# Where a small attention and feed-forward kernel gets its first keys and queries: two of four start-up loads move from the hardware queues to GpSimd's casting queue

## The chip, the cores and the metric

The kernel runs on one core of a Trainium2 chip. A core has a matrix engine (TensorE, "PE" in the profile, with its weight loads as "PEld"), a vector engine (VectorE, "DVE"), an engine for activation functions (ScalarE, "ACT"), a general engine (GpSimd, "POOL") and a synchronising engine (SyncE, "SP"). They run side by side, each through its own instructions in order, and wait for each other through semaphores. Sixteen DMA engines move data between the main memory (HBM) and the on-chip memory (SBUF). A DMA is issued by an engine: by SyncE or ScalarE in what the profile calls a hardware queue (q1 for SyncE, q10 for ScalarE), by GpSimd in the software queue (q0). [...] TensorE writes to PSUM, from where VectorE or ScalarE copy.

The metric is the device time of the whole launch in microseconds (us). Lower is better.

## The reference

Sparse attention over a batch of 4 with 8 heads, 768 positions and head size 64, followed by a feed-forward layer without a residual:

```python
def _attn_ref(q, k, v, n_global, n_local):      # 8 and 96
    scores = scale * np.matmul(q, k.transpose(0, 1, 3, 2))
    rel = pos[:, None] - pos[None, :]
    is_global = pos[None, :] < int(n_global)
    is_local = (rel >= 0) & (rel < int(n_local))
    keep = is_global | is_local
    dist = np.where(is_global & ~is_local, float(n_local), np.abs(rel))
    scores = scores - slopes[:, None, None] * dist[None, :, :]
    scores = np.where(keep, scores, -1000000000.0)
    a = np.exp(scores - np.max(scores, axis=-1, keepdims=True))
    a = a / (np.sum(a, axis=-1, keepdims=True) + 1e-09)
    return np.matmul(a, v)

def _moe_ref(x, w_in, w_out, s, b):             # 3072 x 512, 512 -> 2048 -> 512
    r = np.maximum(x @ w_in, 0.0)
    return (s * (r * r) + b) @ w_out
```

## The kernel before

The tokens are cut into twelve granules of 256 positions (two blocks of 128), three to a batch. A granule goes through attention in units of two heads (four units to a granule; unit `u` is `2` heads of granule `u // 4`), then through the feed-forward layer. Every engine's order of work is written out by hand: the program switches the automatic scheduling off, so that the order of the calls is the order on each engine.

The keys and queries have to be laid out as head size by position before TensorE can use them. The memory gives them as position by head size, so each pair of heads is transposed by TensorE (with an identity matrix, lines 331 and 345) and copied out of PSUM into the tiles `kx` and `qx`.

**The first granule** has a start of its own. Four hardware loads bring its keys and queries in float32 (line 129): SyncE issues the keys and ScalarE the queries, heads 0 to 3 first, then heads 4 to 7, 256 KB each. A partition holds two neighbouring positions, so that each piece read is 512 bytes long. They go into four buffers of the tag `first`. `cast_first(h2, n, copy)` (line 262) turns one of them into bfloat16 and lays it out in the granule's tile `nat[0]`; `h2` is the half of the heads, `n` is 0 for keys and 1 for queries, and `copy` says on which engine, `cp` being VectorE and `acp` ScalarE. `qk_first(h2, n, evac)` (line 325) makes the four transposes of that part, and `evac` copies the result out (line 335).

**All the other loads** are GpSimd's. In the order of their issue: keys and queries of granule 1's first block (`load_qk(1, 0)`), the values of granule 0 (`load_v(0)`, one load to a block), keys and queries of granule 1's second block, and then slices of `w_in` with the values of granule 1 between them, `w_out`, and granules 2 and 3. The issue itself keeps GpSimd busy for most of a microsecond (lines 102, 108, 116, 140 and 146).

**The opening** (lines 1014 to 1048) starts with ten matmuls on constants (`warm`, line 159) while the first loads are on their way. Heads 0 to 3 are cast, transposed and copied out; `open_bias` adds the distance bias of units 0 and 1 by a matmul (line 420), and their scores follow (line 445). Then come the exponentials (`expo`, line 454, on ScalarE), four more warm matmuls, and heads 4 to 7 in the same way for units 2 and 3. After that, granule 1's keys and queries are transposed (line 345), the probabilities are multiplied with the values (`stage_A`, line 499), and the feed-forward layer of granule 0 begins (line 623). `make_koff` (line 387) copies keys for the offset blocks of granule 1.

The scores of units take turns in two PSUM buffers (`sc`), and the transposes and the feed-forward products in three (`psh`). The pool `gpool` has two buffers of the tag `gT`, 16 KB a partition each, which hold the hidden layer of two granules.

Of the kernel before, what the change touches and what calls it, by code (L numbers as in the profile page):

```python
# [8 lines left out]
F32 = mybir.dt.float32  # L9
BF16 = mybir.dt.bfloat16  # L10
# [7 lines left out]
def kernel(  # L18
# [13 lines left out]
    nc = tc.nc  # L32
    P = nc.NUM_PARTITIONS

    B, H, S, D = q.shape
# [4 lines left out]
    GB = 2  # L40
# [17 lines left out]
    work = ctx.enter_context(tc.tile_pool(name="work", bufs=3))  # L58
    ppool = ctx.enter_context(tc.tile_pool(name="ppool", bufs=4))
    gpool = ctx.enter_context(tc.tile_pool(name="gpool", bufs=2))  # L60
# [21 lines left out]
    def nat_tile(j):  # L82
        if j not in nat:
            nat[j] = ldp.tile([P, 2, GB, H, D], BF16, name="nat", tag=f"nat{j % 4}", bufs=1)
        return nat[j]

    srcs = (k, q)

    def rows_of(src, b, sb):
        return src[b, :, sb * P : (sb + 1) * P, :].rearrange("h p d -> p h d")  # L90

    def pairs_of(src, j, h0=0, nh=H):

        b, g = divmod(j, NGR)
        return src[b, h0 : h0 + nh, g * GT : (g + 1) * GT, :].rearrange(
            "h (p s) d -> p h (s d)", s=GB
        )

    def load_qk(j, i):
        b, g = divmod(j, NGR)  # L100
        for n in range(2):
            nc.gpsimd.dma_start(nat_tile(j)[:, n, i, :, :], rows_of(srcs[n], b, g * GB + i))

    def load_v(j, blocks=range(GB)):
        b, g = divmod(j, NGR)
        for i in blocks:
            sb = g * GB + i
            nc.gpsimd.dma_start(vbuf[b % 2][:, sb, :, 0:D], rows_of(v, b, sb))  # L108
# [13 lines left out]
        nc.gpsimd.tensor_copy(g[0:1, :], ap)  # L122


    first_f32 = {}
    for h2 in range(2):
        for n, eng in enumerate((nc.sync, nc.scalar)):
            f = work.tile([P, H // 2, GB * D], F32, name="first", tag="first", bufs=4)
            eng.dma_start(f[:], pairs_of(srcs[n], 0, h2 * H // 2, H // 2))
            first_f32[h2, n] = f  # L130
    nc.scalar.preload_act_table_set("natural_log_exp_and_others")

    w_in_bf = const.tile([P, KC, DF], BF16, name="w_in_bf")
# [22 lines left out]
    def warm(n, w=2 * P):  # L156
        ps = ps_h.tile([P, w], F32, name="ps_w", tag="psh")
        for _ in range(n):
            nc.tensor.matmul(
                ps[:],  # L160
                lhsT=nc.const_aps.tensor(1.0, (P, P), BF16),
                rhs=nc.const_aps.tensor(1.0, (P, w), BF16),
                start=True,
                stop=True,
            )
# [6 lines left out]
        nc.sync.dma_start(b_bc[:], moe_b.to_broadcast((P, 1)))  # L172


    rel_2 = gpool.tile([P, 2, 2 * P], F32, name="rel", tag="gsum2", bufs=1)
    rel, far = rel_2[:, 0, :], rel_2[:, 1, :]
    nc.gpsimd.iota(
# [20 lines left out]
    nc.vector.tensor_scalar_max(base_bf[0:NG, 0, :], base_bf[0:NG, 0, :], -float(NL))  # L198
    nc.vector.memset(base_bf[0:NG, 2, :], -float(NL))
    nat_tile(0)  # L200
    load_qk(1, 0)
    load_v(0)
    load_qk(1, 1)
# [58 lines left out]
    def cast_first(h2, n, copy):  # L262
        hs = slice(h2 * H // 2, (h2 + 1) * H // 2)
        copy(  # L264
            nat[0][:, n, :, hs, :],
            first_f32[h2, n][:].rearrange("p h (s d) -> p s h d", s=GB),
        )


# [6 lines left out]
    gT = {}  # L276
# [6 lines left out]
    def qk_of(b, n):  # L283

        if b not in qk:
            qk[b] = (
                qkp.tile([P, NB, HP, P + (NG + 15) // 16 * 16], BF16, name="kx", tag="kx"),
                qkp.tile([P, NB, HP, P], BF16, name="qx", tag="qx"),
            )
        return qk[b][n][:, :, :, 0:P]  # L290
# [34 lines left out]
    def qk_first(h2, n, evac):  # L325

        ps = ps_h.tile([P, GB, 2, P], BF16, name="ps_t", tag="psh")
        for i in range(GB):
            for c in range(2):
                hp = 2 * h2 + c  # L330
                nc.tensor.transpose(  # L331
                    ps[:, i, c, :], nat[0][:, n, i, 2 * hp : 2 * hp + 2, :], ident_bf[:]
                )
        dst = qk_of(0, n)[:, 0:GB, 2 * h2 : 2 * h2 + 2, :]
        evac(
            dst.rearrange("p b c (m s) -> p c b m s", s=GB),
            ps[:].rearrange("p s c (b m) -> p c b m s", b=GB),
        )
# [534 lines left out]
    def evac(pr, n):  # L873

        ps3 = prod_ps[pr, n][:]
        ps = ps3.rearrange("p a c -> p (a c)")
        if n == 1:
            res[pr] = [
                work.tile([P, GB, CH], F32, name=f"part{i}", tag=f"part{i}", bufs=1)
                for i in range(3)  # L880
            ]
            res[pr].append(out_tile() if pr == NJ // 2 - 1 else res[pr][0])
        r0, r1, r7, r6 = (t[:].rearrange("p a c -> p (a c)") for t in res[pr])
        if n == 1:
            scaled(res[pr][0][:], ps3, both_blocks(bvec[:, 0:CH]))
        elif n == 2:
            store(pr, 0, 0, ps, r0)
        elif n == 5:
            scaled(res[pr][1][:], ps3, both_blocks(bdiff[:]))
        elif n == 6:  # L890
            scaled(r6, ps, r0)
        elif n == 7:
            nc.scalar.activation(r7, ps, ACT.Copy, scale=s_bc[:])
        elif n == 3:
            store(pr, 0, 1, ps, r1)
        elif n == 4:
            store(pr, 1, 0, ps, r6)
# [43 lines left out]
    def run(cs):  # L941
        for c in cs:
            c()
# [54 lines left out]
    cp = nc.vector.tensor_copy  # L998
    acp = nc.scalar.copy
    u = {}  # L1000

    def open_bias(us):
        for i in us:
            u[i] = stage_S(i)
            u[i][0]()
# [7 lines left out]

    warm(10, 4 * P)
    cast_first(0, 0, cp)
    cast_first(0, 1, acp)
    for h in range(6, H):
        nc.vector.tensor_scalar_mul(diag[:, h, :], ident_bf[:], slopes[h] / QSCALE)
    qk_first(0, 0, cp)
    qk_first(0, 1, acp)  # L1020
    open_bias((0, 1))
    cast_first(1, 0, cp)
    cast_first(1, 1, acp)
    for part in range(2):
        for i in (0, 1):
            u[i][1](part)
    run(u[0][2])
    warm(4)
    qk_first(1, 0, cp)
    qk_first(1, 1, acp)  # L1030
    run(u[1][2])
    open_bias((2,))
    open_scores((2,))
    make_koff(1, [0])
# [223 lines left out]
```

The softmax here doesn't subtract the row's maximum and nothing guards it: scores larger than these inputs give would overflow.

## Time and profile before

| | |
|---|---|
| time, median of 6 runs | 208.43 us (208.33 to 208.74) |
| the profiled execution's own time | 208.33 us |
| its span, first to last instruction | 206.5 us |
| granted TensorE clock | 1.00 |
| TensorE / VectorE / ScalarE / GpSimd busy | 202.1 / 160.7 / 128.5 / 69.7 us |
| landing of the four first loads | keys 4.36, queries 4.81; then keys 6.02, queries 6.74 us |
| first packet of GpSimd's queue | 5.58 us (first issue at 1.34) |
| read from HBM, written to it | 27.26 MB, 6.29 MB |

Times within the span are counted from its start. "L264" is line 264 of the kernel. In a group of the profile, `nat<-first` says which tile is written and which is read. A busy TensorE is not TensorE at its peak: matmuls are pipelined and their ends are modelled. The chain of work that ended last is followed back from the last instruction, at each step to whatever released it. A DMA queue's share is the time that its packets took, as a share of 16 engines' time, and packets overlap, so that it can exceed 100%.

### The profile page before, as it was taken

To read this page: it belongs to the slowest core of one execution; us is meant where nothing else is said; L and a number is where in the kernel's file an instruction comes from. 1 tells how busy PE (TensorE), PEld (TensorE's weight loads), DVE (VectorE), ACT (ScalarE), POOL (GpSimd) and SP (SyncE) were. 2 spreads that over 40 slices of the span, in tenths; PEclk is the share of its full clock that TensorE was granted. 3 is DMA by queue.
4 is the path that set the end of the run, shared out by engine and by line. 5 is a ranking of instruction groups with operands and counts; after the bars stand their busy time and mean duration, and the time that the engine had idled before them with its cause. 6 is when DMAs were issued, how large, how long until landed. Compare 5 with 4: busy or idle time off the path is not lost.

```text
span 206.5 us, 5324 instructions
## 1 busy us (share of the span) xinstructions
PE 202.1 (98%) x2192; PEld 160.2 (78%) x2192; DVE 160.7 (78%) x337; ACT 128.5 (62%) x198; POOL 69.7 (34%) x90
## 2 busy tenths in 40 slices
PE   8999999999999999999999999999999999999993
PEld 2678884557867585878888898888888889888883
DVE  7786589977989866799799975699866696737974
ACT  5875669486976558685664595763695764476200
POOL 8985333999355400912700918200000000000000
PEclk9999999999999999999999999999999999999999
DMA  6999999999999999999999999994460300240006
GB/s 166 172 179 201 207 207 177 155 153 136 112 151 135 158 120 229 155 206 237 145 180 164 125 144 214 181 210 57 53 206 3 99 8 0 62 144 0 0 10 197
DMA packets 110836, 28.17 MB, mean 136 GB/s; under 512 B 97852, under 2 KB 109308, under 8 KB 110812
## 3 DMA queue, kind: packets, MB, share of 16 engines
q0 software_dynamic: 76000, 13.11, 86.6%
q1 hardware_dynamic: 33612, 14.13, 39.3%
q10 hardware_dynamic: 1200, 0.59, 1.1%
q8 instruction: 17, 0.28, 0.6%
q14 instruction: 7, 0.06, 0.1%
HBM read 27.26 MB, written 6.29 MB: 162 GB/s over the span
## 4 chain that ended last, share of the span: by engine, by line
PE 96%; DMA 2%; DVE 1%; ACT 0%; issue 0%
PE ps L623 41%; PE ps L823 24%; PE ps L671 14%; PE ps_s L445 6%; PE ps_av L499 5%; DMA first<-in_k_dram 2%; PE ps_t L355 1%; PE ps_s L521 1%; PE ps_x L595 1%; PE ps_s L536 1%; PE ps_t L331 1%; PE ps_av L562 1%; PE ps_t L345 0%; PE ps_s L420 0%; PE ps_last L823 0%; DVE nat L264 0%
## 5 line engine op out<-in xcount | busy, mean ns | idle before, releaser
L623 PE MATMUL ps<-xT,w_in_bf 128*128 128x256 bf16 x768 | 90.3, 273 | 0.0
L633 ACT ACTIVATE gT<-ps 128x512 bf16<-128x512 f32 x96 | 55.8, 599 | 46.7 <-PE ps L623 46.2
L623 PEld LDWEIGHTS <-w_in_bf 128*128 128x128 bf16 x768 | 73.0, 98 | 9.4 <-DVE xT L598 0.2
L454 ACT ACTIVATE pt<-ps_s 128x1024 bf16<-128x1024 f32 (+1 forms) x44 | 39.3, 948 | 2.7 <-PE ps_s L445 2.7
L671 PE MATMUL ps<-w_out_bf,gT 128*128 128x512 bf16 x128 | 29.7, 380 | 0.0
L461 DVE TENSOR_TENSOR pt<-pt,tmpl 128x1024 bf16<-128x1024 bf16 (+1 forms) x40 | 24.5, 646 | 3.6 <-ACT pt L454 3.5
L823 PEld LDWEIGHTS <-gsum 128*128 128x128 bf16 x256 | 24.1, 98 | 3.7 <-DVE gsum L786 0.5
L108 POOL DMA_DIRECT2D vb<-in_v_dram x24 | 21.4, 910 | 5.3 <-DMA w_out_bf<-in_moe_w_out_dram 3.4
L797 DVE TENSOR_TENSOR gT<-gT 128x1024 bf16<-128x1024 bf16 x20 | 13.7, 686 | 11.7 <-ACT gT L633 11.7
L671 PEld LDWEIGHTS <-gT 128*128 128x128 bf16 x128 | 11.7, 98 | 13.0
L470 DVE TENSOR_TENSOR xn<-ps_av,rc 128x256 bf16<-128x256 f32 x48 | 20.4, 425 | 1.7
L823 PEld LDWEIGHTS <-gT 128*128 128x128 bf16 x200 | 18.6, 98 | 2.3
L469 DVE RECIPROCAL rc<-ps_av 128x4 f32<-128x4 f32 x48 | 8.8, 183 | 12.2 <-PE ps_av L499 10.3
L499 PEld LDWEIGHTS <-pt 128*128 128x128 bf16 x320 | 14.4, 97 | 2.7 <-DVE xn L470 0.7
L116 POOL DMA_DIRECT2D nat<-in_k_dram x14 | 12.6, 901 | 8.7 <-DMA nat<-in_k_dram 4.0
L636 DVE TENSOR_TENSOR gT<-gT 128x512 bf16<-128x512 bf16 x32 | 12.8, 421 | 3.5 <-ACT gT L633 3.3
L499 PE MATMUL ps_av<-vb,pt 128*128 128x65 bf16 x208 | 15.4, 193 | 0.0
L823 PE MATMUL ps<-w_out_bf,gsum 128*128 128x256 bf16 x128 | 15.3, 273 | 0.0
L823 PE MATMUL ps<-wsub,gsum 128*128 128x256 bf16 x128 | 15.1, 273 | 0.0
L823 PE MATMUL ps<-w_out_bf,gT 128*128 128x256 bf16 x120 | 13.9, 273 | 0.0
L122 POOL COPY gate<-xT 1x1 bf16<-1x1 bf16 x6 | 1.1, 188 | 37.1 <-DMA xT<-xn 37.1
L116 POOL DMA_DIRECT2D nat<-in_q_dram x14 | 12.4, 886 | 3.0 <-DMA w_in_bf<-in_moe_w_in_dram 1.7
(111 smaller groups left out, 232.0 us busy)
## 6 DMA issues: line engine op xcount, KB each, us to landing
out_dram<-o_q SPq DMA_DIRECT2D x15, 256.0 KB, 2.4
vb<-in_v_dram POOLq DMA_DIRECT2D x24, 128.0 KB, 8.9
nat<-in_k_dram POOLq DMA_DIRECT2D x22, 128.0 KB, 6.7
nat<-in_q_dram POOLq DMA_DIRECT2D x22, 128.0 KB, 6.8
w_out_bf<-in_moe_w_out_dram POOLq DMA_DIRECT2D x4, 512.0 KB, 16.3
w_in_bf<-in_moe_w_in_dram POOLq DMA_DIRECT2D x4, 256.0 KB, 7.5
w_in_bf<-in_moe_w_in_dram POOLq DMA_DIRECT2D x2, 512.0 KB, 11.5
out_dram<-o_sb SPq DMA_DIRECT2D x4, 256.0 KB, 6.9
```

Source lines behind the costliest of these rows:

```text
L108: nc.gpsimd.dma_start(vbuf[b % 2][:, sb, :, 0:D], rows_of(v, b, sb))
L116: nc.gpsimd.dma_start(t[:, n, i, :, :], rows_of(srcs[n], b, sb))
L454: nc.scalar.activation(pt[:, :, 0:ncol], ps[:, :, 0:ncol], ACT.Exp, scale=QSCALE)
L461: nc.vector.tensor_tensor(pv, pv, m.rearrange("p h a c -> p h (a c)"), ALU.mult)
L470: nc.vector.tensor_tensor(dst, av[:, :, :, 0:D], rc[:].to_broadcast((P, 2, 2, D)), ALU.mult)
L499: nc.tensor.matmul(av[:, i, hi, 0 : D + 1], lhsT=pt[:, hi, c * P : (c + 1) * P], rhs=vv, start=(n == 0), stop=(n == len(terms) - 1),)
L623: nc.tensor.matmul(ps[:, i, :], lhsT=w_in_bf[:, kc, fc * P : (fc + 1) * P], rhs=xT[j][:, kc, :], start=(kc == 0), stop=(kc == KC - 1),)
L633: nc.scalar.activation(gs, ps[:], ACT.Relu)
L636: nc.vector.tensor_tensor(gs, gs, gs, ALU.mult)
L671: nc.tensor.matmul(po[:], lhsT=g_of(j)[:, fc, tb * P : (tb + 1) * P], rhs=w_out_bf[:, fc, :], start=(fc == 0), stop=(fc == FC - 1),)
L797: outs.append(lambda: nc.vector.tensor_tensor(gs, gs, gs, ALU.mult))
L823: nc.tensor.matmul(ps[:, tb, cs], lhsT=stat[:, fc, tb * P : (tb + 1) * P], rhs=mov[:, fc, cs], start=(fc == 0), stop=(fc == NH - 1),)
```

## The change

The keys and queries of heads 4 to 7 of the first granule no longer come by the hardware queues. GpSimd loads them with two casting DMAs, ahead of all its other loads, as bfloat16 into a tile `later`, which takes one of the two `gT` buffers. The layout in it is the loads' own (head, then two positions), so `cast_first` for this half is a copy from bfloat16 to bfloat16; both copies are VectorE's now, and so are both copies of the transposes out of PSUM. The exponential of unit 1 is called ahead of them, and the four warm matmuls are split into two ahead of the transposes and two behind.

```diff
-    first_f32 = {}
-    for h2 in range(2):
-        for n, eng in enumerate((nc.sync, nc.scalar)):
-            f = work.tile([P, H // 2, GB * D], F32, name="first", tag="first", bufs=4)
-            eng.dma_start(f[:], pairs_of(srcs[n], 0, h2 * H // 2, H // 2))
-            first_f32[h2, n] = f
+    first_half = {}
+    for n, eng in enumerate((nc.sync, nc.scalar)):
+        f = work.tile([P, H // 2, GB * D], F32, name="first", tag="first", bufs=4)
+        eng.dma_start(f[:], pairs_of(srcs[n], 0, 0, H // 2))
+        first_half[0, n] = f[:]
+    later = gpool.tile([P, 2, H // 2, GB * D], BF16, name="later", tag="gT")
+    for n in range(2):
+        first_half[1, n] = later[:, n]
...
+    def load_later():
+        for n in range(2):
+            nc.gpsimd.dma_start(later[:, n], pairs_of(srcs[n], 0, H // 2, H // 2))
...
     nat_tile(0)
+    load_later()
     load_qk(1, 0)
     load_v(0)
...
             nat[0][:, n, :, hs, :],
-            first_f32[h2, n][:].rearrange("p h (s d) -> p s h d", s=GB),
+            first_half[h2, n].rearrange("p h (s d) -> p s h d", s=GB),
...
     open_bias((0, 1))
     cast_first(1, 0, cp)
-    cast_first(1, 1, acp)
     for part in range(2):
         for i in (0, 1):
             u[i][1](part)
     run(u[0][2])
-    warm(4)
+    run(u[1][2])
+    cast_first(1, 1, cp)
+    warm(2)
     qk_first(1, 0, cp)
-    qk_first(1, 1, acp)
-    run(u[1][2])
+    qk_first(1, 1, cp)
+    warm(2)
     open_bias((2,))
```

## The prediction

> **What bounds the kernel now.** I read the page first. TensorE is busy for 98% of the span, and the chain of work that ended last is 96% TensorE. So nothing can be won or lost except where TensorE waits, and the second view, the chain in order of time, says where that is: only ahead of 8.9 us.
>
> ```profile
> span 206.5 us, 5324 instructions
> PE 202.1 (98%) x2192; PEld 160.2 (78%) x2192; DVE 160.7 (78%) x337; ACT 128.5 (62%) x198; POOL 69.7 (34%) x90
> PE 96%; DMA 2%; DVE 1%; ACT 0%; issue 0%
> ```
>
> The same chain, cut to 4.3 to 10.5 us (start, length, what):
>
> ```profile
> 4.38 0.88 DVE nat L264
> ...
> 5.30 0.76 PE ps_t L331 x8
> 6.06 0.65 PE ps_s L420 x4
> ...
> 6.74 0.51 PE ps_s L445 x12
> 7.25 0.55 PE ps_w L159 x4
> 7.80 0.46 PE ps_t L331 x8
> ...
> 8.28 0.59 ACT qx L335
> ...
> 8.92 0.34 PE ps_s L445 x6
> ```
>
> Three things other than TensorE stand in it: the landing of the first keys (4.36) with VectorE's cast of them, and ScalarE's copy of the second half's queries, which ends at 8.87 and lets unit 2's scores start at 8.92. From there to the end the chain is TensorE's alone: a delay at 8.92 goes to the end in full, and an earlier start does too, if the data come.
>
> The third view is the queues. GpSimd's queue (q0) feeds everything after the first loads, and is the tight resource. Two stretches of the DMA view, 5.0 to 5.5 and then 5.5 to 6.1 us (packets, MB, share):
>
> ```profile
> q10 hardware_dynamic: 227, 0.12, 96.7%
> q1 hardware_dynamic: 70, 0.03, 25.6%
> ```
> ```profile
> q0 software_dynamic: 320, 0.04, 106.5%
> q10 hardware_dynamic: 199, 0.09, 67.4%
> ```
>
> GpSimd issues its first load at 1.34, yet q0 moves nothing before 5.58. ScalarE's q10 closes its last load on the 16 engines one by one from 5.58 to 6.03, and q0 starts on each just then. From there q0 has no gap over 0.4 us before 81 us. Its landings are just in time: the second block of values lands at 10.27 (issue 4.09 plus 6.18) and TensorE's first use is at 10.42; block 1's queries land at 11.91 for 12.00; the fourth eighth of w_in at 19.52 for 19.72. A q0 stream later by more than about 0.1 us stalls TensorE.
>
> The fourth view is the timeline of VectorE beside GpSimd:
>
> ```profile
> 3.23 1.77 POOL L108 DMA_DIRECT2D vb<-in_v_dram  x2
> ...
> 5.83 0.92 POOL L102 DMA_DIRECT2D nat<-in_q_dram  x1
> ```
> ```profile
> 4.38 0.86 DVE L264 CAST nat<-first 128x512 bf16<-128x512 f32 x1 [0.25 <-DMA first<-in_k_dram]
> ...
> 6.48 0.52 DVE L264 CAST nat<-first 128x512 bf16<-128x512 f32 x1
> ```
>
> The same cast takes 0.86 and 0.52. Both end 0.25 after GpSimd's running issue ends (4.99 and 6.75): a copy from SBUF to SBUF that starts well inside an issue waits for its end. Those starting less than 0.24 into one do not wait (line 197, 0.20).
>
> **The change, part by part.** The sum is made against the profiled execution: span 206.5, time 208.33, so 1.83 lies around it; it is 0.10 under the median of 208.43, which I add at the end.
>
> *The two hardware loads of heads 4 to 7 go.* Their packets ran from 4.0 to 6.03. The first two loads close at 3.52 to 3.88 (keys) and 3.90 to 4.26 (queries), before or just as the removed ones begin, so I leave their landings at 4.36 and 4.81. ScalarE's issue of 0.61 goes too; its table load comes 0.6 sooner, but it then waited 0.35 for the queries anyway: nothing.
>
> *Two casting loads ahead in q0.* Each has 512 packets of 256 B. q0 moved 619 packets of 128 B in 0.5 us (0.81 ns each), and 116 of 512 B in 0.3 (2.59 ns). Between them, 256 B comes to 1.40 ns, 0.72 us a load and 1.44 for both. The ends are 0.83 and 2.65 for both. q0 can start when ScalarE's first load closes, at 3.90 to 4.26 instead of 5.58 to 6.03: 1.7 sooner. Everything behind in q0 (keys and queries of granule 1, values, w_in, w_out) moves by 1.44 - 1.70 = -0.26, ends -0.87 and +0.95. I take -0.26; being early is worth nothing, as TensorE is not waiting for it.
>
> *Issues on GpSimd.* Two more, 0.74 each (the w_in issues of as many pieces start 0.74 apart, 6.70 to 7.44) and 0.15 for the first, as now (1.34 to 2.36 where others take 0.87). All later issues move by 1.63. The fourth load behind them (values) is then issued at 5.58; with 1.58 from issue to first packet (114.15 to 115.73, where q0 was empty) it could move from 7.2, and its turn comes at 8.0: hidden by 0.8. If that cover went, each 0.1 would come out at the values' use.
>
> *Landing of the later half.* q0 takes 0.76 from a load's last closing packet (6.88) to its landing (7.64). Keys: 4.26 + 0.72 + 0.76 = 5.74, queries 6.46. VectorE is busy until 6.5, so neither is waited for.
>
> *First cast.* GpSimd's issues now start at 1.34, 2.23, 2.97, 3.84 and 4.71. The cast of the first keys starts at 4.38, well inside the fourth, and ends 0.25 after 4.74, at 4.99 instead of 5.25. The keys' transposes come 0.25 sooner; the queries' do not (cast on ScalarE to 5.45), so scores 0 and 1 start some 0.14 sooner, at 6.60. Ends: 0 and -0.35.
>
> *Two layout copies on VectorE instead of a cast each on VectorE (0.52) and ScalarE (0.62).* 128x512 bf16 to bf16: 0.28 alone and 0.47 with a wait (line 387). They run from 6.3 to at most 7.4, while TensorE does scores 0 and 1 and the warm matmuls to about 7.3: hidden. Ending 0.3 later, they would push what follows one for one.
>
> *Warm matmuls 2 and 2 instead of 4.* Two fewer ahead of the transposes: 2 x 0.114 = -0.23. The two behind run while TensorE waits for the copies: nothing.
>
> *Both copies out of PSUM on VectorE.* Line 335 takes 0.69 there (0.59 on ScalarE), and now one follows the other. Before: the keys' transposes end at 8.02, ScalarE ends at 8.87. After: scores at 6.60 + 0.44 to the warm matmuls + 0.23 + 0.38 for the keys' transposes = 7.65; + 0.04, 0.61 and 0.69 = 8.99; unit 2's scores at 9.04. That is **+0.12** against 8.92, and +0.26 if the first cast gains nothing. Behind them on VectorE wait make_koff and granule 1's copies, which end by 10.5; block 1's use of them is at 11.25.
>
> *ScalarE.* The exponential of unit 1 moves from 8.76 to about 8.0; bias and scores of unit 3 did not wait for it: nothing.
>
> **Sum:** 208.33 + 0.12 + 0.10 = 208.55. Its own range, by the ends of the first cast and of the copies, is 208.25 to 208.85. No change means within 0.2%, 0.42 us, about what a measurement of this kernel can tell.
>
> [...] The trace shows q0 waiting until the hardware queues have emptied. [...]
>
> **The rivals.**
> *R1, q0's start is its own latency.* Then 5.58 stays, and the new loads put 1.44 on everything behind. The values land at 11.7, and the later queries near 7.9, so that unit 2 starts about 0.7 late and the values' use moves to 11.15. TensorE stalls there, and the total is about +1.2: 209.6. It decides from a start over 0.5 later than I take (0.26, and 0.27 of slack behind it). For it: nothing of q0 moves in 4.2 us. Against it: the start follows each engine's close. Chance 0.12.
> *R2, the casting loads cost as much as 512 B packets* (2.65 for both). The values land 0.95 late, against 0.15 of slack and 0.12 of TensorE's own delay: +0.8, 209.2. For it: they read 512 B pieces. Chance 0.10.
> *R3, the first half lands sooner.* From 2.3 to 2.8 the queues moved 63 packets, at 65 GB/s, where 3.5 to 3.9 has 341. If the loads queued second cause that gap, both landings come some 0.5 to 0.9 sooner, scores 0 and 1 start as much sooner, less 0.26 for the copies: 207.95 to 208.2. Against it: VectorE is not free before 3.9. Chance 0.15, two thirds of it beyond the bound.
> *R4, the port.* A layout copy that starts inside an issue waits up to 0.6 for its end, and the copies behind it slip: +0.5, 208.95. Chance 0.06.
>
> **How the numbers follow.** The forecast has 0.57. Faster by over 0.2% is R3's 0.10. Slower is R1, R2 and R4: 0.28. The rest, 0.62, is within 0.2%. The range goes from R3's 208.0 to 209.3 above R2, and leaves out R1 and a little of R3, under 0.2.
>
> **What would show it.** q0's first packet near 4.0, granule 1's landings 0.1 to 0.4 sooner, the first cast ending near 5.0, line 335 twice on VectorE back to back, and unit 2's scores at about 9.04 with no idle TensorE at the first line 499. A first packet at 5.6, or TensorE waiting at line 499, makes it wrong upward; landings of the first keys before 4.1, downward.

## The result

| | before | after |
|---|---|---|
| time, median | 208.52 us (43 runs) | 209.19 us (21 runs) |
| spread | 208.23 to 209.87 us | 208.62 to 210.03 us |
| profiled execution: time, span | 208.33, 206.5 us | 209.21, 207.4 us |
| unit 2's scores start | 8.92 us | 9.49 us |
| first keys, first queries land | 4.36, 4.81 us | 4.38, 4.85 us |
| keys, queries of heads 4 to 7 land | 6.02, 6.74 us | 6.16, 6.91 us |
| GpSimd's queue (q0) starts | 5.58 us | 3.81 us |

The changed kernel takes 1.0032 times as long (95% interval 1.0023 to 1.0041): 0.67 us more. This is slower, by little more than the 0.42 us that I called no change. The forecast of 208.55 was 0.64 us too low, and the result lies inside the range.

The page of the changed kernel still shows TensorE all but alone on the chain that ended last:

```profile
span 207.4 us, 5324 instructions
PE 202.7 (98%) x2192; PEld 160.3 (77%) x2192; DVE 162.1 (78%) x339; ACT 127.5 (61%) x196; POOL 71.1 (34%) x92
...
PE 97%; DVE 1%; issue 0%
```

The chain of the changed kernel in order of time (start, length, what), over the same stretch as shown of before:

```profile
5.20 0.95 PE ps_t L338 x8
6.16 0.96 PE ps_s L427 x4
7.12 0.44 PE ps_s L452 x12
7.56 0.33 PE ps_w L161 x2
7.88 0.24 PE ps_t L338 x4
8.12 0.02 issue
8.14 0.69 DVE kx L342
8.84 0.61 DVE qx L342
9.45 0.04 issue
9.49 0.34 PE ps_s L452 x6
```

The landing of the first keys is no longer a link. The two copies out of PSUM now stand one after the other (8.14 to 9.45), where before ScalarE's single copy stood (8.28 to 8.87). And the first links are longer than in the profile of before, though the instructions are the same: the four bias matmuls (`ps_s`, 128 x 384) take 0.96 instead of 0.65, the eight transposes 0.95 instead of 0.76. In this execution the trace's record of the full TensorE clock begins at 6.65 us, in that of before at 5.62.

The queues of the changed kernel, 3.5 to 4.0 and then 4.5 to 5.0 us (packets, MB, share):

```profile
q10 hardware_dynamic: 275, 0.14, 92.1%
q1 hardware_dynamic: 64, 0.03, 18.2%
q0 software_dynamic: 12, 0.00, 6.1%
```
```profile
q0 software_dynamic: 307, 0.08, 158.6%
```

q0 starts as q10's only load closes, 1.78 us sooner than before. But its 256-byte packets then come at 307 in half a microsecond, 1.63 ns each, and from 5.0 to 5.5 at 262, 1.91 ns each. With 1,024 of them, q0 needs about 1.8 us for the two loads.

TensorE's start times in the two profiles, instruction by instruction, differ by +0.57 at 8.9 us, +0.75 from 14.8 us and +0.79 from 83 us to the end. So in this pair of executions nearly all of the loss is made in the first 15 us: 0.57 in the opening and 0.17 at the first feed-forward product, which had to wait for VectorE. VectorE and GpSimd of the changed kernel at that place (start, length, what):

```profile
12.91 1.60 POOL L142 DMA_DIRECT2D w_in_bf<-in_moe_w_in_dram  x2
...
13.98 0.64 DVE L394 COPY ko<-kx 128x512 bf16<-128x512 bf16 x1
...
14.77 0.74 DVE L605 COPY xT<-ps_x 128x512 bf16<-128x512 bf16 x2
```

The second `make_koff` copy took 0.28 before:

```profile
13.41 0.28 DVE L387 COPY ko<-kx 128x512 bf16<-128x512 bf16 x1
```

It started 0.24 into an issue and did not wait. Here it starts 0.35 into GpSimd's second issue, which ends at 14.51, and ends 0.11 after it; the copies of `xT`, which the feed-forward product needs, stand behind it. All GpSimd's issues come 1.5 to 1.6 us later than before, so that VectorE's copies meet other ones, and at other points.

One pair of profiles can't say what of this is the change and what is that execution's. The experiments are about that.

### The profile page after: what moved, and what is told of

It reads as the page before. It is cut to its first block, busy times and chain, and to the rows that moved or that the text cites. A ratio compares the mean times of both kernels' runs of the same rounds, so it can differ in the third digit from the quotient of the medians.

```text
span 207.4 us, 5324 instructions
## 1 busy us (share of the span) xinstructions
PE 202.7 (98%) x2192; PEld 160.3 (77%) x2192; DVE 162.1 (78%) x339; ACT 127.5 (61%) x196; POOL 71.1 (34%) x92
## 4 chain that ended last, share of the span: by engine, by line
PE 97%; DVE 1%; issue 0%
PE ps L630 41%; PE ps L830 24%; PE ps L678 14%; PE ps_s L452 6%; PE ps_av L506 5%; PE ps_w L161 2%; PE ps_t L362 1%; PE ps_s L528 1%; PE ps_x L602 1%; PE ps_s L543 1%; PE ps_s L427 1%; PE ps_av L569 1%; PE ps_t L338 1%; PE ps_t L352 0%; PE ps_last L830 0%; DVE kx L342 0%
## 5 line engine op out<-in xcount | busy, mean ns | idle before, releaser
L122 POOL COPY gate<-xT 1x1 bf16<-1x1 bf16 x6 | 1.7, 276 | 35.9 <-DMA xT<-xn 35.9
```

## The experiments

The theories at the start: **A**, the loss is made by the order and the engines of the opening (with the clock, and with a copy's wait for GpSimd's issue, 0.64 instead of 0.28, which the expectation below calls a wait at a port), and the loads cost nothing; **B**, the place of the loads in q0 costs. Each run lists its median and its ratio to the kernel before, run beside it on the same chip. "Shift" is the difference of TensorE's start times from those of the kernel compared, in the profiled executions.

### The loads alone

The changed kernel's loads, tile and buffers, with the opening as it was before (copies on VectorE and ScalarE, `warm(4)`).

```diff
     nat_tile(0)
+    load_later()
     load_qk(1, 0)
...
-            first_f32[h2, n][:].rearrange("p h (s d) -> p s h d", s=GB),
+            first_half[h2, n].rearrange("p h (s d) -> p s h d", s=GB),
```

> The two casting loads ahead in GpSimd's queue as in the change, but engines and order of the opening as before it: the second queries' cast and copy on ScalarE, four warm matmuls ahead of the transposes, unit 1's exponential last. Theory A (the loss is in the order of the opening, in the TensorE clock and in one wait at GpSimd's port; the loads cost nothing): unit 2's scores start within 0.15 us of the 8.92 of before once the moment of the clock's grant is taken off, and the time is 208.5 to 208.75. Rival B (the place of the loads in GpSimd's queue costs, through later issues and landings): 208.9 to 209.2, as after the change.

Measured: 209.39 us (before 208.49), ratio 1.0038 (1.0026 to 1.0050). Theory A's "the loads cost nothing" falls: alone they cost at least as much as the whole change, and more than rival B's 208.9 to 209.2. The opening is hardly later (unit 2's scores +0.08). The shift grows where TensorE waits for data: to +0.19 at the values' first use (they land 0.30 later), and from +0.30 to +0.87 at 83 us. TensorE there, in this kernel's profile and then in that of the changed kernel:

```profile
82.11 1.46 PE L678 MATMUL ps<-w_out_bf,gT 128*128 128x512 bf16 x6
83.96 0.60 PE L630 MATMUL ps<-xT,w_in_bf 128*128 128x256 bf16 x4 [0.40 <-DMA xT<-xn]
```
```profile
82.11 1.90 PE L678 MATMUL ps<-w_out_bf,gT 128*128 128x512 bf16 x8
83.88 0.60 PE L630 MATMUL ps<-xT,w_in_bf 128*128 128x256 bf16 x4
```

The transposed inputs `xT` land at 83.83 here and at 83.75 in the changed kernel, which needs them only at 83.88. In the kernel before they land at 82.48, for a use at 83.09.

The step between these two, 0.11 at 59 us, is not data. The small `make_koff` copy there starts inside one of GpSimd's issues and takes 0.56, where it took 0.18 in the kernel before, and the scores on its result wait for it:

```profile
58.66 0.88 POOL L108 DMA_DIRECT2D vb<-in_v_dram  x1
58.95 0.56 DVE L395 COPY ko<-kx 128x64 bf16<-128x64 bf16 x1
```

### The order alone

The four hardware loads of before, with the changed kernel's calls in the opening.

```diff
     cast_first(1, 0, cp)
-    cast_first(1, 1, acp)
...
     run(u[0][2])
-    warm(4)
-    qk_first(1, 0, cp)
-    qk_first(1, 1, acp)
     run(u[1][2])
+    cast_first(1, 1, cp)
+    warm(2)
+    qk_first(1, 0, cp)
+    qk_first(1, 1, cp)
+    warm(2)
```

> Four hardware loads as before, with the change's order alone: both casts and both copies of the second half on VectorE, unit 1's exponential ahead, warm matmuls two and two. Theory A: both copies in a row cost 0.26 at unit 2's scores, which start near 9.2, and GpSimd's issues stand where they stood, so nothing is added at make_koff near 14 us: 208.75 to 208.9. Rival B: 208.4 to 208.6, no change.

Measured: 208.86 us (208.49), ratio 1.0017 (1.0006 to 1.0027). Unit 2's scores start 0.22 later, as theory A had it; the `make_koff` copy meets an issue here too (0.62), and that adds 0.14. Its chain, with the copies back to back:

```profile
7.53 0.24 PE ps_t L331 x4
7.77 0.02 issue
7.79 0.69 DVE kx L335
8.48 0.61 DVE qx L335
9.09 0.04 issue
9.13 0.34 PE ps_s L445 x6
```

### The change without the late copy

The second `make_koff` copy of granule 1 as a maximum of the tile with itself, the same values by another VectorE operation.

```diff
-        nc.vector.tensor_copy(ko[:, i0 : i0 + n], kx[:, lo : lo + n, :, 0:P])
+        src = kx[:, lo : lo + n, :, 0:P]
+        if j == 1 and blocks == [1]:
+            nc.vector.tensor_tensor(ko[:, i0 : i0 + n], src, src, ALU.max)
+        else:
+            nc.vector.tensor_copy(ko[:, i0 : i0 + n], src)
```

> The changed kernel with one copy replaced: the second make_koff of granule 1 takes the larger of its source and the same source, an operation of two inputs that takes 0.42 us and does not wait for a GpSimd issue; the copy took 0.64 in the changed kernel and 0.28 in the one before. Theory A: xT's copy behind it comes 0.2 sooner, the wait inside the first feed-forward product (0.10) goes, and the time falls by about 0.1 to 209.05 to 209.1. Rival B: no change from 209.2.

```profile
13.70 0.41 DVE L396 TENSOR_TENSOR ko<-kx 128x512 bf16<-128x512 bf16 x1
14.15 0.33 DVE L399 COPY ko<-kx 128x32 bf16<-128x32 bf16 x1
14.23 0.75 DVE L609 COPY xT<-ps_x 128x512 bf16<-128x512 bf16 x2
```

It takes 0.41 and does not wait, and the step of 0.17 is gone from the shift. But it also starts 0.28 sooner than the copy of the changed kernel did, 0.06 into GpSimd's issue (13.64 to 14.48) and not 0.3, and the copy of before, 0.24 into its issue, did not wait. So its place alone could have saved it. But the operation would have too: the squares of line 636 in the kernel before also read two inputs in SBUF, and the ten of them that start 0.34 to 0.72 into an issue take 0.41 to 0.42, the seventeen outside an issue 0.41 to 0.43. The time, 209.05 us (ratio 1.0035, 1.0022 to 1.0048, 5 runs), can't be told from that of the changed kernel. This profile also bears on the question of the clock: the opening is the changed kernel's to the instruction, the full clock is recorded from 3.96 us, scores 0 start at 6.76 instead of 7.05, and unit 2's scores at 9.20, +0.29. That is not yet the change's share of the 0.57 above, as the first queries land at 5.00 in this execution, and landed at 4.85 in the other. The next kernel has the same opening up to scores 0; its queries land at 4.84, its full clock is recorded from 5.12, and its scores 0 start at 6.61. So I estimate that some 0.44 of the 0.57 was that execution's late clock (7.05 to 6.61) and some 0.13 is the change's, and that 0.15 of the 0.29 here comes with the later landing.

### The change with the queries' copy on ScalarE

```diff
     run(u[0][2])
-    run(u[1][2])
     cast_first(1, 1, cp)
     warm(2)
     qk_first(1, 0, cp)
-    qk_first(1, 1, cp)
+    qk_first(1, 1, acp)
+    run(u[1][2])
     warm(2)
```

> The changed kernel with the second queries' copy out of PSUM back on ScalarE and unit 1's exponential behind it; the loads, both casts on VectorE and the warm matmuls stay. Theory A: the copy starts when unit 0's exponential ends and unit 2's scores start 0.4 sooner than the changed kernel's: 208.75 to 208.9. Rival B: 209.0 to 209.2.

Measured: 209.34 us, ratio 1.0040 (1.0022 to 1.0058), more than both forecasts. The opening did what it should: unit 2's scores start at 8.61, 0.30 sooner than before and 0.87 sooner than in the changed kernel. Nothing of it is left at the end (+1.45 in the profile, an execution of 209.88 us and so one of the longer ones). The shift climbs at one use after another: 0.12 at the values, 0.19 at granule 1's second queries, 0.21 at the `make_koff` copy, 0.23 at 39 us, 0.48 at 59 us and 0.53 at `xT` (the step at `make_koff` is VectorE's, not the stream's). This is where a new theory began, **S**: two chains race, TensorE's opening and the stream of loads. Whichever is later at a use decides, and the changed kernel makes both a little later.

### One load more in front of the stream

The kernel before, with one more casting load first in q0, into a buffer that nothing reads. Opening and hardware loads are untouched.

```diff
     nat_tile(0)
+    spare = gpool.tile([P, H // 2, GB * D], BF16, name="spare", tag="gT")
+    nc.gpsimd.dma_start(spare[:], pairs_of(srcs[0], 0, H // 2, H // 2))
     load_qk(1, 0)
```

> The kernel before with one more casting load ahead of all others in GpSimd's queue: the keys of heads 4 to 7 (512 packets of 256 B) into a spare buffer that nothing reads. The four hardware loads stay. It adds about 0.8 to 0.9 us (half of the 1.8 that the two casting loads took in the changed kernel) to everything behind it in GpSimd's queue, and touches no other engine's order. Theory S (the loss is the stream's: granule 1's values, its later queries, w_in and the transposes of granule 4 come just in time): the values land at about 11.1 instead of 10.3, TensorE stalls there by some 0.5 to 0.8 us, and the time is 209.0 to 209.3, against 208.5. Rival O (the loss is the opening's order of copies alone, and the stream has room): the landings are later and nothing waits; 208.5, within 0.1 of the kernel before.

Measured: 209.15 us (208.54), ratio 1.0031 (1.0016 to 1.0045), as theory S had it. The values land at 11.17 instead of 10.27. TensorE, in the kernel before and then here:

```profile
10.35 0.54 PE L499 MATMUL ps_av<-vb,pt 128*128 128x65 bf16 x12
```
```profile
10.47 0.24 PE L501 MATMUL ps_av<-vb,pt 128*128 128x65 bf16 x2
11.21 0.46 PE L501 MATMUL ps_av<-vb,pt 128*128 128x65 bf16 x10 [0.50 <-DMA vb<-in_v_dram]
```

The shift is +0.13 ahead of it, +0.79 behind it, and +0.78 at the end. So 0.9 us of delay in q0 costs 0.6 to 0.7 us, in this profile all of it at one use. GpSimd's later issues slide by 0.9 us too, but no step of the shift lies at a copy that met one.

### The same kernels with a relieved stream

Three kernels without the keys and queries of granule 1's second block, which is then computed from the first block's data: the kernel before, the loads alone, and the version with ScalarE's copy.

```diff
-    load_qk(1, 1)
...
-                    ps[:, hp, :], nat[j][:, n, i, 2 * hp : 2 * hp + 2, :], ident_bf[:]
+                    ps[:, hp, :], nat[j][:, n, 0, 2 * hp : 2 * hp + 2, :], ident_bf[:]
```

> The kernel before without the loads of the keys and queries of granule 1's second block (its part of the computation is done with the first block's data, so the output is another one). It takes 512 KB, some 1.75 us, out of GpSimd's queue from about 10 us on. It is the base for the two kernels beside it. Theory S: the stalls of the kernel before that the stream causes are few, since it is just in time, so it gains little: 208.1 to 208.5. Rival O: 208.5, no change. So it alone tells little; what counts is how the next two stand to it.

> The changed kernel's two casting loads with the engines and the order of the kernel before, and likewise without the loads of granule 1's second block. With these loads in, moving the two loads cost 0.9 us against the kernel before (209.39 to 208.49). Theory S: that was the stream's lateness; with 1.75 us taken out of it the loss is gone from 12 us on, what stays is the stall at the values' first use (about 0.1): within 0.2 us of the kernel without those loads beside it. Rival O: the place of the loads costs by itself, in the opening, whatever follows: it stays 0.6 to 0.9 us above that kernel.

> The changed kernel with the queries' copy out of PSUM on ScalarE and unit 1's exponential behind it, and likewise without the loads of granule 1's second block. With those loads in it had unit 2's scores 0.3 us sooner than the kernel before and yet took 209.34, as the data came late. Theory S: with the stream relieved the sooner opening counts, and it ends 0 to 0.3 us below the kernel before without those loads. Rival O: the opening isn't what sets the end; it stays 0.5 to 0.9 us above.

Measured: 208.32, 208.69 and 208.97 us, that is +0.37 and +0.65 to the first of them, where with those loads it was +0.90 and +0.85. For the loads alone both theories miss; for the version with ScalarE's copy theory S misses, and rival O's figure (0.5 to 0.9 above) is met. The stall at `xT` is gone, but the one at the values is not 0.1, as I expected: the shift rises there by 0.47 and 0.52. The loads alone were profiled in one of their longer executions (209.16 us). TensorE in them, relieved:

```profile
10.32 0.24 PE L505 MATMUL ps_av<-vb,pt 128*128 128x65 bf16 x2
10.86 0.47 PE L505 MATMUL ps_av<-vb,pt 128*128 128x65 bf16 x10 [0.30 <-DMA vb<-in_v_dram]
```

The second block of values lands at 10.81 and 10.83 in these two, against 10.21 in the kernel beside them. Until then q0 was not late: in the loads alone the keys, the queries and the first block of values land at 7.55, 8.42 and 9.38, against 7.84, 8.65 and 9.51 in the kernel beside them. The second block then takes 1.43 more instead of 0.70. Why is not settled. By the medians ScalarE's copy gains nothing over the loads alone here either (208.97 to 208.69). The profile can't say more of it, as unit 2's scores start only 0.06 sooner in it than in the kernel beside: its full clock is recorded from 5.99, the other's from 3.77.

### The stream relieved ahead of the second stall

Three kernels without the values of the second batch's last granule (GpSimd writes ones in their place).

```diff
-    load_v(5)
+    nc.gpsimd.memset(vbuf[1][:, 2 * GB : 3 * GB, :, 0:D], 1.0)
```

> The kernel before without the loads of the values of the last granule of the second batch (GpSimd writes ones there instead, so the output is another one). It takes 512 KB, some 1.75 us, out of GpSimd's queue at about 61 to 64 us, where the queue runs some 10 us behind its issues, and so lets everything behind it, the feed-forward inputs of the third granule by DMA transposes (needed at 83.1) among them, come sooner. It is the base for the two beside it. The kernel before had 0.6 us of slack there, so it gains little: 208.3 to 208.5.

> The changed kernel's two casting loads with the engines and the order of the kernel before, likewise without the values of that granule. With them, moving the two loads cost 0.9 us, of which its profile put 0.2 to 0.3 at the values' first use (10.4 us) and 0.57 at the DMA-transposed inputs (83 us). Theory S (two separate stalls of a stream that comes just in time): the second goes and the first stays, 0.2 to 0.45 above the kernel beside it. Rival O (what was seen at 83 us is a coincidence of one profile, the cost is made in the opening): 0.8 to 0.9 above.

> The changed kernel likewise without the values of that granule. In its own profile all of the loss lies in the opening (0.57 at unit 2's scores, of which 0.3 came with a later clock grant, and 0.17 at the first feed-forward product), and none at 83 us, yet its times spread from 208.6 to 210.0. Theory S: the upper part of that spread is the stall at 83 us, which some executions have; without it the times are 208.6 to 209.3, median 0.4 to 0.6 above the kernel without those loads. Rival O: the spread and the median stay, 0.7 above.

Measured: 208.36, 209.45 and 209.30 us. Theory S in the form "two stalls, at 10.4 and 83 us" falls: the figures are above rival O's, +1.09 and +0.94. `xT` now lands at 81.81 in the loads alone and at 81.30 in the changed kernel, and nothing waits for it, yet the loads alone stay 1.09 above the kernel beside them, and the changed kernel keeps its spread (208.54 to 210.28). The opening, where rival O put the cost, is not it either: it is only 0.08 later in the loads alone. Their shift against the kernel beside them grows at other uses of data: +0.25 at 12.0, +0.26 at 39.1, +0.32 at 59.0. What ended the first of these waits, in the chain of this kernel:

```profile
7.32 5.15 DMA nat<-in_q_dram
12.47 0.05 issue
12.52 0.40 PE ps_t L352 x4
```

These are granule 1's second queries, which land at 12.47 for a use at 12.3; those of the kernel beside it land at 12.11. So the loads alone lost time at data in all three of their profiles, at other uses each time: 10.4 and 83 us; 10.4 us; 12, 39 and 59 us. Most of the rest of the first two shifts was lost at `make_koff` copies that met an issue: 0.11 at 59 us in the first, as shown, and 0.26 at 41 us in the second (0.70 and 0.62 for its two copies, 0.83 and 0.18 in the kernel beside it). Of the changed kernel's own order, three profiles (as it is, without the late copy, and here) show no stall at data beyond 0.2, and were executions of 208.83 to 209.21 us. A profile of it above 209.3 was not caught, so what its slowest executions wait for is open.

## Why the prediction was right or wrong

**The range: partly luck.** I gave 0.62 to no change and 0.28 to slower, and slower it was. That 209.19 lies inside the range owes much to its upper end, 209.3, which stood there for R2. What R2 says, casting loads of 2.65 us and values that land 0.95 late, did not come: the values landed at 10.36 instead of 10.27. The time came from terms that the sum had at nothing or too small.

**q0's start: right.** I said 3.90 to 4.26, as q10's load closes; it was 3.81 to 4.24. R1 (own latency, 5.58) falls. The landings of the first half, unchanged, were right too (4.38 and 4.85), so R3 falls.

**The price of the two casting loads: mis-sized.** I took 1.40 ns a packet, 1.44 us for both, half-way between the 128 B and the 512 B packets; they cost 1.6 to 1.9 ns, about 1.8 us. That is within the range given (0.83 to 2.65), a third of the way to R2. With the start 1.78 sooner, this price alone brings my -0.26 to about nothing, and that is what q0's packets show right behind the loads: counted without the moved loads, its first 0.1 MB is written 0.02 sooner than before. The lateness builds up behind, +0.07 at 0.25 MB and +0.13 at 0.75 MB: from 6 to 10 us q0 writes 0.59 MB, and 0.62 before. Why it is slower there, no run here shows. Its first 1.5 MB is written at 14.85 in before, 0.19 later in the changed kernel, 0.21 in the loads alone, 0.88 with one load more, and 0.02 in the order alone. The sum of what the loads take is what hardly moved: 2.0 us on the hardware queues before (4.0 to 6.03), 1.8 on q0 after.

The row for that was there, and I read only the gap it would leave. In these two profiles the first hardware loads lost nearly nothing to the casting loads: between 3.5 and 4.0 us q0 moved 12 packets and q10 275, and the first landings are 0.02 and 0.04 later.

**"Being early is worth nothing": incomplete.** I priced what an earlier stream gains and gave lateness only to the rivals, though I had written that 0.1 us of lateness stalls TensorE. With +0.1 to +0.2 in place of -0.26, single loads come later by more (the first slice of w_in by 0.53), and the loads alone cost 0.9 us. This is the largest term that failed. In the full change it shows less: 0.37 for the order and 0.90 for the loads make 0.67 together, not 1.27. A likely reason, argued and not shown, is that the later opening moves TensorE's uses back as well.

**The opening: the mechanism was right, one term holds only at times.** From scores 0 to unit 2's scores I counted 2.44 us (6.60 to 9.04): the changed kernel, the one without the late copy and the order alone show 2.43 to 2.44. The copies of line 342 stand back to back at 0.69 and 0.68. The first cast ended at 5.01 (predicted 4.99). "Scores 0 and 1 start 0.14 sooner, at 6.60" holds where the first queries land as early as in the profile that I worked from (4.81): with ScalarE's copy they landed at 4.84, and scores 0 started at 6.61. Where they land at 5.00, the queries set the start and not the keys, and nothing is gained: 6.76 without the late copy, 6.77 in the changed kernel without the last granule's values. In the changed kernel's own profile the bias matmuls ran ahead of the record of the full clock (6.65) and took 0.96 instead of 0.65: they start 0.32 apart there (5.95, 6.27, 6.59), and 0.16 apart behind it (8.41, 8.57) and in the profile of before (5.90 to 6.39, record from 5.62). So scores 0 started at 7.05. Over the changed kernel's three profiles and the five others with its loads the landing varies from 4.84 to 5.06. So +0.12 and +0.26, the figure that I gave for no gain from the first cast, are both true, each of some executions, and I had priced one execution's landing. The layout copies waited for the queries (0.32, as these landed at 6.91 and not at 6.46), and were hidden as said.

**The clock: not in the sum.** Over the thirteen profiles of this study the record of the full clock begins anywhere from 3.77 to 6.65 us, with the same ten warm matmuls ahead. What sets the moment, no run here shows. A single profile of this opening can thus carry an estimated 0.4 us that belongs to no kernel (the 7.05 to 6.61 of scores 0).

**R4: the wait came, its price at another place.** A layout copy was hit: the second starts 0.48 into an issue, takes 0.56 and ends 0.11 after it, and the first, late in the issue before, takes 0.30.

```profile
6.31 0.30 DVE L271 COPY nat<-later 128x512 bf16<-128x512 bf16 x1
6.45 0.93 POOL L102 DMA_DIRECT2D nat<-in_k_dram  x1
6.93 0.56 DVE L271 COPY nat<-later 128x512 bf16<-128x512 bf16 x1 [0.32 <-DMA later<-in_q_dram]
```

Without the late copy both were hit (0.52 and 0.77). It cost nothing, as TensorE came to the second copy's result only at 7.94 and 7.66; the +0.5 of R4 left out this cover. The second `make_koff`, 7 us further on, had no cover and cost 0.17 in the changed kernel. In the order alone, where no new load pushes the issues back, it cost 0.14: the later opening alone moved the copy from 0.24 to 0.32 into its issue. I had called the later issues "hidden by 0.8", looking only at the data that they fetch, not at which copies they would meet. That copy waited (0.64 inside an issue, 0.28 before), and the two-input squares did not (0.41 to 0.42 inside an issue, 0.41 to 0.43 outside). The port in R4's name was my guess at the cause, which no run here shows.

## What to carry to other kernels

The transfers that moved to another queue took their time along (2.0 us before, 1.8 after). Add such a time to the stream that is joined, and ask of every later use how much slack it has there, before asking what the place left free gains. Where loads came just in time, an opening that was 0.3 us sooner and a stream that was 0.2 us later made a slower kernel. A term read from one profile may be that execution's: look at the same landing in a second one. When a queue of issues slides, check which of VectorE's copies from SBUF to SBUF the issues now meet, all along the program: here one took 0.64 instead of 0.28.

## What was unexpected of the hardware

- 256-byte packets of a casting load cost 1.6 to 1.9 ns, 128-byte packets 0.81: in bytes per time the larger ones gained nothing (134 to 157 GB/s against 158).
- One load more in q0 moved the whole stream behind it by a constant 0.86 to 0.89 us up to 35 us; the order of landings made it neither larger nor smaller.
- The same two loads come out at different uses in the three profiles of the loads alone (two of them with other loads taken out), with stalls at data of 0.1 to 0.6, and in the sum 0.7 to 0.9 us, of which 0.1 and 0.3 in two of them at copies that met an issue.
